# Splitting the first channel-mix weight's later parts into halves without TensorE, in a new order of work

## The chip, the cores and the metric

The kernel runs on one core of a Trainium2 chip. Its time is device time in microseconds (us) of one execution. Five engines work side by side, each through its own queue, in the order in which the program was built: PE (TensorE, matmul), DVE (VectorE), ACT (ScalarE), POOL (GpSimd) and SP, which here issues the transfers. PEld is the weight load of a matmul, which overlaps the matmul before it.

## The reference, cut to what matters

```python
# 1. linear attention with a decaying state, heads of 48, 768 steps, 4 batches
y[t] = r[t] @ (state + outer(u * k[t], v[t]));  state = w[t] * state + outer(k[t], v[t])
# 2. four experts of causal attention on x [4, 768, 384], the best two mixed by a gate
out += gate_e * softmax(mask((x@wq[e]) @ (x@wk[e]).T / 8)) @ (x@wv[e]) @ wo[e]
# 3. channel mix, what the change is about: w_ch1 is [384, 1536], w_ch2 is [1536, 384]
xn = (x - mean) / sqrt(var + 1e-6) * g_ln
return x + maximum(xn @ w_ch1, 0) @ w_ch2
```

## The kernel before, in words

Every large product is made of three float16 products: a float32 operand is scaled by a power of two and split into a high half (`hi`, the value rounded to float16) and a low half (`lo`, the rest), and hi x hi, hi x lo and lo x hi are summed. So the two channel-mix weights, w1 (w_ch1) and w2 (w_ch2), have to be split once, before the first block of rows can be multiplied by them.

Rows are worked in chunks of 128 (6 in each of 4 batches). A chunk passes the linear attention (`rwkv_chunk`), the projections of its batch (`project`, L1124, and L1145, which takes the high half off again in PSUM), the scores (L1303, their exponentials split by L1361 on ACT and L1365 on DVE), the sum over values (L1388), the output projection (L1440, copied out by L1453) and then, in blocks of two chunks, the norm (`norm`: L1494 makes the high half on ACT, L1498 the low one on DVE, L1505 transposes both by DMA into a tile called xnT) and the channel mix (`mlp`: L1533 multiplies by w1 into a tile called pm, L1544 and L1548 split the result, L1566 multiplies by w2 into pz, L1573 adds it to the rows). Block (0,0) is the first of twelve. In the names, numbers behind a tile are batch, chunk or buffer.

The weights arrive as 64-bit words. `big_weights` takes w1 in four groups of three parts and w2 in six groups of two; a part is 128x384. A group is loaded (L553) into a ring that later carries rows: w1 into the three slots of the ring of x1, the rows themselves (its tile is printed as x or x1_69), so that a group fills the ring, and w2 into the two slots of xnT. Three integer operations on DVE turn its words into float32 (`unpack`, L505 to L507). ACT then squares it for the largest value (`top`, L576). The scales of all weights come from the first groups alone, in one chain of small steps (`was`; their tile is s_all_False, and for w1 gsFalse).

From there a part can go two ways. By **TensorE**, for all of w1 and for w2's first group: PE multiplies the float32 part by a diagonal matrix of scales (`times`, L656, which goes over the data in two passes), ACT copies the product out as the high half (`hi`, L660), PE takes that off in PSUM (`less`, L664), ACT copies out the low half (`lo`, L668). The ring slot is free after `top`. Or **direct**, for the other five groups of w2: the decoded float32 words stay in the ring slot, ACT makes the high half from them (L633), and one DVE operation with two inputs from SBUF makes the low half (L637). Here the slot is free only after that `lo`.

The order of the work isn't that of the text: every step is recorded with its engine, an assumed duration, what it comes after and which ring slot it takes and frees, and a planner (`Plan.order`) lays the steps out. Of the steps that could start within `LOOK` it takes the one with the lowest `due`, plus `LATE` times the delay; `due` is a sum of numbers from the table `PLACE`, by step and by group. While PE would stand idle early on, the planner puts in dummy matmuls (`spin`, L745), ruled by `UNTIL`, `SPAN`, `LEAST` and `GAP`. What the planner lays out is then fixed in each engine's queue. A second copy of the steps behind it serves inputs that the fast one can't hold; it isn't run here.

```python
direct = which in PRM["DIRECT"] and k > 0 and not safe
```

is the line that chooses the way of group k.

## Time and profile before

| | |
|---|---|
| three runs | 624.44, 626.21, 627.24 us (median 626.21) |
| profiled execution | 624.58 us, of which span 622.9 us |
| PE busy | 591.2 us (95%) |
| DVE busy | 431.1 us (69%) |
| ACT busy | 386.8 us (62%) |
| POOL busy | 153.9 us (25%) |
| mean granted clock of PE | 0.997 |

The span is the time from the first to the last recorded instruction; 1.7 us of the execution lie outside it. A busy share is a mean over stages: here the first fifth of the span, in which the weights are split and the first chunks go through all stages, looks different from the rest, so the stretches have to be read apart.

### The profile page before, as it was taken

To read this page: it belongs to the slowest core of one execution; us is meant where nothing else is said; L and a number is where in the kernel's file an instruction comes from. 1 tells how busy PE (TensorE), PEld (TensorE's weight loads), DVE (VectorE), ACT (ScalarE), POOL (GpSimd) and SP (SyncE) were. 2 spreads that over 40 slices of the span, in tenths; PEclk is the share of its full clock that TensorE was granted. 3 is DMA by queue.
4 is the path that set the end of the run, shared out by engine and by line. 5 is a ranking of instruction groups with operands and counts; after the bars stand their busy time and mean duration, and the time that the engine had idled before them with its cause. 6 is when DMAs were issued, how large, how long until landed. Compare 5 with 4: busy or idle time off the path is not lost.

```text
span 622.9 us, 16217 instructions
## 1 busy us (share of the span) xinstructions
PE 591.2 (95%) x6560; PEld 438.1 (70%) x6560; DVE 431.1 (69%) x817; ACT 386.8 (62%) x1059; POOL 153.9 (25%) x179
## 2 busy tenths in 40 slices
PE   6689888799999999999999999999999999999996
PEld 3566655577688867767777776777876768687783
DVE  6979898879898679689973689765564645442230
ACT  6298879966775686777646778655484745543120
POOL 5525233425453125055530045100000000000000
PEclk9999999999999999999999999999999999999999
DMA  8744674695986476699764579646238354532000
GB/s 279 266 145 162 196 183 138 132 246 114 181 229 141 94 143 175 125 214 243 146 124 97 96 196 180 102 73 124 48 43 178 69 114 75 98 65 59 14 15 29
DMA packets 151138, 83.32 MB, mean 134 GB/s; under 512 B 123664, under 2 KB 136720, under 8 KB 151056
## 3 DMA queue, kind: packets, MB, share of 16 engines
q1 hardware_dynamic: 151056, 82.21, 57.2%
q8 instruction: 53, 0.87, 0.6%
q14 instruction: 29, 0.24, 0.1%
HBM read 42.34 MB, written 4.72 MB: 76 GB/s over the span
## 4 chain that ended last, share of the span: by engine, by line
PE 72%; DVE 11%; ACT 9%; DMA 4%; issue 2%; SPq 1%; POOL 0%; ACTq 0%; DVEq 0%
PE pz L1566 21%; PE pm L1533 21%; PE pq L1124 6%; PE ps L1303 5%; PE po L1388 4%; PE pa L919 3%; PE px L1440 3%; PE py L969 2%; PE pv L1189 2%; DMA xnT<-in_w_dram 2%; PE py L955 2%; ACT ps L1345 2%; DMA seq<-in_seq_dram 1%; DVE hl L1365 1%; PE pd L984 1%
## 5 line engine op out<-in xcount | busy, mean ns | idle before, releaser
L1566 PE MATMUL pz<-w_w,hid 128*128 128x384 f16 x864 | 151.8, 326 | 0.0
L1533 PE MATMUL pm<-xnT,w_w 128*128 128x256 f16 x1296 | 150.9, 274 | 0.5 <-DVE hid L1548 0.5
L1533 PEld LDWEIGHTS <-w_w 128*128 128x128 f16 x1296 | 124.8, 98 | 19.7 <-issue 3.7
L1566 PEld LDWEIGHTS <-hid 128*128 128x128 f16 x864 | 81.5, 98 | 50.7 <-issue 2.0
L1544 ACT ACTIVATE hid<-pm 128x512 f16<-128x512 f32 x72 | 42.6, 593 | 62.3 <-PE pm L1533 62.3
L1365 DVE SCALAR_TENSOR_TENSOR hl<-ps,hl 128x512 f16<-128x512 f32 (+2 forms) x68 | 54.6, 811 | 35.1 <-ACT hl L1361 34.5
L1548 DVE SCALAR_TENSOR_TENSOR hid<-pm,hid 128x512 f16<-128x512 f32 x72 | 49.2, 685 | 37.0 <-ACT hid L1544 36.6
L1482 POOL TENSOR_TENSOR rs_y<-rs_v,half 128x2 f32<-128x2 f32 x12 | 8.4, 700 | 218.5 <-ACT rs_v L1478 218.5
L892 POOL TENSOR_SCALAR_AFFINE_SELECT am<-cb 128x512 f32<-128x512 f32 x48 | 44.7, 954 | 60.8 <-DVE cb L878 37.7
L1124 PE MATMUL pq<-xT,w_qk 128*128 128x256 f16 x432 | 50.8, 273 | 0.0
L1361 ACT ACTIVATE hl<-ps 128x512 f16<-128x512 f32 (+2 forms) x68 | 46.6, 694 | 1.3 <-DMA pt<-hl 0.4
L1124 PEld LDWEIGHTS <-w_qk 128*128 128x128 f16 x432 | 41.4, 98 | 7.7 <-issue 2.0
L1345 ACT ACTIVATE ps<-ps,bias 128x640 f32<-128x640 f32 (+1 forms) x32 | 26.2, 819 | 29.5 <-DVE ps L1316 27.9
L863 POOL TENSOR_TENSOR tok<-tok 128x384 f32<-128x384 f32 x19 | 22.5, 1182 | 84.9 <-DMA tok<-in_tok_dram 84.9
L1388 PEld LDWEIGHTS <-pt 128*128 128x128 f16 x1008 | 37.1, 98 | 5.2 <-issue 0.8
L834 POOL TENSOR_TENSOR rp<-seq,fw 128x512 f32<-128x512 f32 x24 | 31.5, 1313 | 36.1 <-DVE fw L817 34.1
L1388 PE MATMUL po<-vt,pt 128*128 128x64 f16 x1008 | 39.6, 193 | 0.2 <-DMA pt<-hl 0.2
L1345 ACT ACTIVATE ps<-ps,bias,scales 128x128 f32<-128x128 f32 (+3 forms) x64 | 37.7, 589 | 1.8
L1316 DVE TENSOR_SCALAR_CACHE_REDUCE ps<-ps,scales 128x640 f32<-128x640 f32 (+1 forms) x32 | 30.4, 951 | 11.7 <-PE ps L1306 11.4
L1573 DVE SCALAR_TENSOR_TENSOR x<-pz,ioutFalse,x 128x384 f32<-128x384 f32 x24 | 14.7, 613 | 31.9 <-PE pz L1566 31.8
L802 DVE TENSOR_TENSOR_SCAN bw<-seq,starts 128x516 f32<-128x516 f32 x24 | 35.4, 1476 | 0.8 <-DMA seq<-in_seq_dram 0.6
L926 DVE COPY_PREDICATED am<-above,pa 128x512 f32<-128x512 int8 x48 | 33.1, 719 | 0.3
(225 smaller groups left out, 1062.1 us busy)
## 6 DMA issues: line engine op xcount, KB each, us to landing
seq<-in_seq_dram SPq DMA_DIRECT2D x48, 256.0 KB, 4.6
tok<-in_tok_dram SPq DMA_DIRECT2D x19, 384.0 KB, 3.9
seq<-in_seq_dram SPq DMA_DIRECT2D x24, 258.5 KB, 3.3
seq<-in_seq_dram SPq DMA_DIRECT2D x24, 192.0 KB, 4.9
xnT<-in_w_dram SPq DMA_DIRECT2D x6, 768.0 KB, 4.9
x<-in_w_dram SPq DMA_DIRECT2D x4, 1152.0 KB, 7.2
out_dram<-x SPq DMA_DIRECT2D x24, 192.0 KB, 2.4
xk<-kd SPq DMA_DIRECT2D x16, 192.0 KB, 3.3
```

The costliest lines, as they stand in the source:

```text
L802: V.tensor_tensor_scan(t["bw"][:, NP * CW : 0 : -1], t["wT"][:, NP * CW : 0 : -1], starts[:, NP * CW : 0 : -1], 0.0, op0=OP.mult, op1=OP.max)
L892: G.affine_select(out=t["am"][:, j], in_=t["cb"].rearrange("p (h j) -> p h j", j=2)[:, :, j, None].to_broadcast([P, NP, P]), compare_op=OP ...
L926: V.copy_predicated(t["am"][:, j], above[:, None, :].to_broadcast([P, NP, P]), t["pa"][j].rearrange("p (h t) -> p h t", t=P))
L1124: T.matmul(h["pq"][:, :n].rearrange("p (c t) -> p c t", t=P), wt["qk"][:, lw, kk, mt * P : (mt + 1) * P], t["xT", c0 // 2][:, :, lx * KK + ...
L1345: A.activation(ps, ps, AF.Exp, bias=h["bias"][:, e : e + 1], scale=-1.0 if alone else t["x"]["esc"], accum_out=r["sums"][:, e : e + 1])
L1361: A.activation(part(u, heads, 0, W), view(heads, h, W, spot), AF.Copy, scale=2.0 ** 14)
L1365: V.scalar_tensor_tensor(out=part(u, heads, half_at, W), in0=view(heads, h, W, spot), scalar=2.0 ** 14, in1=part(u, heads, 0, W), op0=OP.m ...
L1388: T.matmul(r["po"][:, e * HD : (e + 1) * HD], u["pt"][:, (lp * len(heads) + k) * (i + 1) + kb, :], t["vt"][:, kb, lv, e * HD : (e + 1) * H ...
L1533: T.matmul(h["pm"][:, j * 256 : (j + 1) * 256].rearrange("p (c t) -> p c t", t=P), wt["w1"][:, KK * (f // 3) + kk, lw, f % 3 * P : (f % 3 ...
L1544: A.activation(hid[fp][:, 0], h["pm"], AF.Relu)
L1548: V.scalar_tensor_tensor(out=hid[fp][:, 1], in0=h["pm"], scalar=0.0, in1=hid[fp][:, 0], op0=OP.max, op1=OP.subtract)
L1566: T.matmul(h["po"][:, :DM], hid[fp][:, lh, c0 : c0 + P], wt["w2"][:, 2 * fp + j, lw, :], start=(fp + j + i == 0), stop=(fp == NF // 2 - 1 ...
```

## The change

One entry of the parameters, `DIRECT`, now names w1 as well as w2. So w1's groups 1 to 3, nine parts, go the direct way: nine L656 pairs and nine L664 on PE and nine L660 and nine L668 on ACT are gone, nine L633 on ACT and nine L637 on DVE are new. Group 0 of w1 and of w2 stay with TensorE. The three slots of x1 are now held until the low halves of a group are made, where `top` freed them before. All other parameters of the planner and every number of `PLACE` are different too, so that each engine's queue has a new order. Line numbers behind the table are one lower in the changed kernel (L637 is L636 there).

```diff
-PRM = dict(LOOK=0.0326, LATE=14146.9836, UNTIL=35.809, SPAN=5.4007, LEAST=0.144, GAP=2.97, LAND=2.3828, NPA=6, NQ=1, NCB=5, DIRECT=('w2',), NST=5)
+PRM = dict(LOOK=0.0, LATE=1150.6432, UNTIL=44.1537, SPAN=2.789, LEAST=0.6368, GAP=2.61, LAND=2.2113, NPA=6, NQ=1, NCB=5, DIRECT=('w1','w2'), NST=5)
 PLACE = {
-    ('av', 0, 0): -158057.83, ('av', 0, 1): -232158.2, ('av', 0, 2): -102859.22, ('av', 0, 3): -263757.53,
...
```

Counted over the program's main part, PE has 18 dummy matmuls (L745) where it had 10; apart from the steps named so far every engine has the same instructions as before.

The first place is ACT's queue around the first copy of finished rows into x1 (L1453 before, L1452 after; px is the output projection). Before, part 2, 3 and 9 of w1 are on their way through PSUM there (w1_ps is the PSUM tile of `times`):

```order
L660 ACTIVATE w_w1_132<-w1_ps2_False_1234 128x384
L1453 ACTIVATE x1_69,mv_0_0_1287<-px_0_0_1264,scales_0_351 128x384
L660 ACTIVATE w_w1_132<-w1_ps3_False_1256 128x384
L1457 ACTIVATE mv_0_0_1287<-mv_0_0_1287 128x1
L1461 ACTIVATE spare_128,mv_0_0_1287<-x1_69,mv_0_0_1287 128x384
L812 ACTIVATE decay_120<-bw_1_0_1289 128x4
L668 ACTIVATE w_w1_132<-w1_ps2_False_1234 128x384
L1330 ACTIVATE bias_0_2_0_1330<-top_0_2_0_1306,scales_0_351 128x2
L668 ACTIVATE w_w1_132<-w1_ps3_False_1256 128x384
L1345 ACTIVATE ps_0_2_0_1278,sums_0_2_1335<-ps_0_2_0_1278,bias_0_2_0_1330,scales_0_351 128x384 x2
L660 ACTIVATE w_w1_132<-w1_ps9_False_1333 128x384
```

and now the queue has group 3's square (`top`) and its three high halves ahead of that copy, and nothing from PSUM of w1:

```order
L575 ACTIVATE w_w1_132,w1_maxFalse_136<-x1_69 128x1152
L1195 ACTIVATE vt_0_780<-pv_0_4_1234 128x256
L632 ACTIVATE w_w1_132<-x1_69,gsFalse_424 128x384
L1199 ACTIVATE lg_0_138<-pv_0_4_1234,scales_0_362 128x4
L822 ACTIVATE seq_0_5_910,sums_117<-seq_0_5_910,shift_118 128x4x128
L632 ACTIVATE w_w1_132<-x1_69,gsFalse_424 128x384 x2
L1329 ACTIVATE bias_0_2_0_1285<-top_0_2_0_1274,scales_0_362 128x2
L1344 ACTIVATE ps_0_2_0_1251,sums_0_2_1287<-ps_0_2_0_1251,bias_0_2_0_1285,scales_0_362 128x384 x2
L1360 ACTIVATE hl_0_2_0_1305<-ps_0_2_0_1251 128x768
L1452 ACTIVATE x1_69,mv_0_0_1307<-px_0_0_1264,scales_0_362 128x384
```

What moved: the PSUM copies of w1 that stood before, between and behind the copies into x1 are gone, and the three high halves stand ahead of the first copy, since x1's slots hold the group until its low halves are made.

The second place is DVE's queue at the same point. Before, DVE is done with w1 after its last decode (L507 into w_w1) and goes on to a group of w2 (L505 to L507 from xnT):

```order
L507 SCALAR_TENSOR_TENSOR w_w1_132<-x1_69,w_w1_132 128x1152
L1365 SCALAR_TENSOR_TENSOR hl_0_1_2_1107<-ps_0_1_2_1042,hl_0_1_2_1107 128x512
L505 TENSOR_SCALAR w_w2_133<-xnT_70 128x768
L1076 SCALAR_TENSOR_TENSOR xT_0_2_1116<-py_0_4_1003,scales_0_351,xT_0_2_1116 128x384
L1406 RECIPROCAL den_0_1_1114<-den_0_1_1114 128x4
L1407 TENSOR_TENSOR den_0_1_1114<-den_0_1_1114,gw_0_855 128x4
L808 RECIPROCAL begin_100<-bw_0_5_1092 128x4
L506 SCALAR_TENSOR_TENSOR w_w2_133<-xnT_70,w_w2_133 128x768
L507 SCALAR_TENSOR_TENSOR xnT_70<-xnT_70,w_w2_133 128x768
```

and now the three low halves of group 3 stand in one row ahead of the split of chunk 2's exponentials (hl_0_2_0):

```order
L1320 TENSOR_REDUCE top_0_2_0_1274<-ps_0_2_0_1251 128x2
L678 TENSOR_REDUCE sane_134<-w1_maxFalse_136 128x1
L680 TENSOR_SCALAR sane_134<-sane_134,g_peakFalse_135 128x1
L681 TENSOR_SCALAR sane_134<-sane_134,s_all_False_415 128x1
L682 TENSOR_SCALAR sane_134<-sane_134 128x1
L636 SCALAR_TENSOR_TENSOR w_w1_132<-x1_69,gsFalse_424,w_w1_132 128x384 x3
L801 SCALAR_TENSOR_TENSOR bw_1_0_1303<-seq_1_0_1199,starts_71 128x516
L1364 SCALAR_TENSOR_TENSOR hl_0_2_0_1305<-ps_0_2_0_1251,hl_0_2_0_1305 128x768
```

What moved: sixteen low halves (seven of w2 and nine of w1) now stand ahead of the low half of block (0,0)'s norm (L1498, L1497 after) where nine of w2 stood, and one group of w2 fewer is decoded ahead of it: nine groups instead of ten.

The third place is SP's queue. Before, the last group of w2 is loaded (L553, from in_w2) ahead of the transposes of chunk 2 and of block (0,0)'s rows (L1505):

```order
L553 DMA xnT_70<-in_w2_dram 128x768
L1429 DMA_TRANSPOSE oT_0_1_1291<-o16_0_1_1273 128x4x128
L773 DMA seq_1_1_1366<-in_seq_dram 128x517
L797 DMA tok_1_1_1379<-in_tok_dram 128x768
L781 DMA seq_1_1_1366<-in_seq_dram 128x512
L785 DMA seq_1_1_1366<-in_seq_dram 128x512
L1374 DMA_TRANSPOSE pt_0_2_0_1402<-hl_0_2_0_1361 128x12x128
L789 DMA seq_1_1_1366<-in_seq_dram 128x384
L1374 DMA_TRANSPOSE pt_0_2_2_1475<-hl_0_2_2_1453 128x12x128
L1505 DMA_TRANSPOSE xnT_70<-x16_0_0_1501 128x12x128
```

and now that load stands behind them, among the transposes of chunks 3 and 4, and waits for PE, since block (0,0)'s xnT has to be read out of the slots first:

```order
L784 DMA seq_1_3_1869<-in_seq_dram 128x512
L788 DMA seq_1_3_1869<-in_seq_dram 128x384
L1373 DMA_TRANSPOSE pt_0_4_0_1987<-hl_0_4_0_1946 128x10x128
L1428 DMA_TRANSPOSE oT_0_3_2015<-o16_0_3_1993 128x4x128
L552 DMA xnT_70<-in_w2_dram 128x768
L1373 DMA_TRANSPOSE pt_0_4_1_2100<-hl_0_4_1_2047 128x10x128
```

What moved: the last group of w2 is loaded, decoded and split after the last L1533 of block (0,0) instead of ahead of its first.

## Rows read from the trace of the kernel before

**Rows 1.** The page: busy time, share and instructions of each engine.

```profile
PE 591.2 (95%) x6560; PEld 438.1 (70%) x6560; DVE 431.1 (69%) x817; ACT 386.8 (62%) x1059; POOL 153.9 (25%) x179
```

**Rows 2.** Busy time by stretch (start:end length, PE, PEld, DVE, ACT, POOL, clock, DMA).

```profile
0.00:122.64 122.64, 98.71 (x996) 67.72 (x997) 105.94 (x214) 93.93 (x293) 50.67 (x61) 1.00 0.62 188
122.64:617.98 495.34, 492.48 (x5564) 370.35 (x5563) 325.11 (x603) 292.86 (x767) 103.28 (x118) 1.00 0.57 121
...
67.46:115.03 47.57, 39.78 (x461) 25.61 (x461) 43.20 (x84) 41.83 (x122) 17.99 (x19) 1.00 0.59 160
115.03:157.00 41.97, 39.61 (x515) 29.64 (x513) 34.87 (x62) 29.06 (x79) 14.38 (x15) 0.96 0.77 173
124.00:128.00 4.00, 4.00 (x41) 1.98 (x43) 3.47 (x7) 0.95 (x3) 0.00 (x0) 0.60 0.92 206
```

**Rows 3.** What PE waited for behind the first L1533: total, times, longest.

```profile
PE ps L1303 <- DVE hl L1365: 0.9, 3, 0.4
```

**Rows 4.** Timeline of block (0,0)'s way to PE, and the last L1573.

```profile
115.03 0.96 DVE L1498 TENSOR_TENSOR x<-xn,x 128x768 f16<-128x768 f32 x1 [0.17 <-ACT x L1494]
...
122.64 0.27 PE L1145 MATMUL pq<-kd,minus 128*128 128x256 f16 x1 [2.01 <-ACT kd L1138]
...
122.75 1.57 PE L1533 MATMUL pm<-xnT,w_w 128*128 128x256 f16 x11
...
617.36 0.62 DVE L1573 SCALAR_TENSOR_TENSOR x<-pz,ioutFalse,x 128x384 f32<-128x384 f32 x1 [5.23 <-PE pz L1566]
```

**Rows 5.** Groups by line and form: busy us, mean ns, idle before.

```profile
L656 PE MATMUL w_ps_False<-w_w,diag_w_False 128*128 128x384 f32 x24 | 9.8, 505 | 0.3 <-ACT w_w L668 0.3
...
L664 PE MATMUL w_ps_False<-w_w,minus 128*128 128x384 f16 x14 | 4.3, 327 | 1.2 <-ACT w_w L660 1.0
...
L633 ACT ACTIVATE w_w<-xnT,s_all_False 128x384 f16<-128x384 f32 x10 | 6.4, 654 | 0.0
...
L660 ACT ACTIVATE w_w<-w_ps_False 128x384 f16<-128x384 f32 x14 | 7.1, 518 | 0.5 <-PE w_ps_False L656 0.5
...
L637 DVE SCALAR_TENSOR_TENSOR w_w<-xnT,s_all_False,w_w 128x384 f16<-128x384 f32 x10 | 5.8, 609 | 1.4 <-ACT w_w L633 1.4
...
L505 DVE TENSOR_SCALAR w_w<-xnT 128x768 int32<-128x768 int32 x6 | 4.3, 712 | 5.8 <-DMA xnT<-in_w_dram 5.8
...
L506 DVE SCALAR_TENSOR_TENSOR w_w<-xnT,w_w 128x768 int32<-128x768 int32 x6 | 6.0, 1000 | 0.1
...
L507 DVE SCALAR_TENSOR_TENSOR xnT<-xnT,w_w 128x768 int32<-128x768 int32 x5 | 5.5, 1110 | 0.1
...
L802 DVE TENSOR_TENSOR_SCAN bw<-seq,starts 128x516 f32<-128x516 f32 x24 | 35.4, 1476 | 0.8 <-DMA seq<-in_seq_dram 0.6
```

**Rows 6.** Timeline of two PE pieces of the split.

```profile
84.45 1.46 PE L656 MATMUL w_ps_False<-w_w,diag_w_False 128*128 128x384 f32 x4
...
90.67 0.33 PE L664 MATMUL w_ps_False<-w_w,minus 128*128 128x384 f16 x1
```

**Rows 7.** What DVE waited for up to 115 us: total, times, longest.

```profile
DVE w_w L505 <- DMA xnT<-in_w_dram: 5.8, 2, 3.4
DVE w_w L637 <- ACT w_w L633: 1.4, 1, 1.4
```

**Rows 8.** The page, issues: KB each, us to landing.

```profile
xnT<-in_w_dram SPq DMA_DIRECT2D x6, 768.0 KB, 4.9
```

**Rows 9.** Timeline: two DVE operations with and without POOL beside them.

```profile
30.31 0.96 DVE L507 SCALAR_TENSOR_TENSOR xnT<-xnT,w_w 128x768 int32<-128x768 int32 x1
...
76.99 0.61 DVE L637 SCALAR_TENSOR_TENSOR w_w<-xnT,s_all_False,w_w 128x384 f16<-128x384 f32 x1
...
77.36 1.09 POOL L873 TENSOR_TENSOR tok<-tok,u_sb 128x384 f32<-128x384 f32 x1 [0.37 <-DMA u_sb<-in_ub_dram]
...
89.00 1.00 POOL L863 TENSOR_TENSOR tok<-tok 128x384 f32<-128x384 f32 x1 [3.98 <-DMA tok<-in_tok_dram]
...
89.10 1.72 DVE L507 SCALAR_TENSOR_TENSOR xnT<-xnT,w_w 128x768 int32<-128x768 int32 x1
```

51 lines of the change are left out of this document (25 added, 26 removed), and 79 rows, old and new, of the table PLACE.

## The prediction, made before the changed kernel had run

> **What bounds the kernel now.** I read the page's busy line first: PE 591.2 us of 622.9, DVE 431.1, ACT 386.8 [rows 1]. That mean hides two stages, so I cut the span where TensorE starts its first L1533, at 122.64 us, and where the last result is added, at 617.98 (a start of 617.36 and 0.62 of length) [rows 4]. Behind the cut PE is busy 492.48 us of 495.34; ahead of it only 98.71 of 122.64 [rows 2]. The list of PE's waits says the same of the later stage: the largest is 0.9 us in all, on DVE's L1365 [rows 3]. So from 122.64 us on the time is PE's work, and the change has nine parts less of that only if they stand there. Ahead of it PE has 24 us of holes, and the question is what lets the first L1533 start.
>
> That is the way of block (0,0): DVE's low half L1498 at 115.03, the transposes, then L1533 at 122.75, right behind an L1145 for which PE had idled 2.01 us [rows 4]. On the way to L1498 I compare DVE and ACT: from 67.46 us (the first low half of the exponentials) to 115.03 DVE is busy 43.20 of 47.57 us, ACT 41.83 and PE 39.78 [rows 2]. DVE is the fullest there, with 4.4 us idle, and ACT follows close behind. So a step taken from PE or ACT helps as far as DVE waited for it, and a step given to DVE costs its whole length.
>
> **Removed, PE.** Two parts by L656 took 1.46 us, with a tail of pipeline in it [rows 6]; by the means, a pass starts while the last one drains, and I count 0.65 us a part, 0.16 for L664 (half of the 0.33 that one takes alone with its tail [rows 6]): 9 x 0.81 = 7.3 us. All nine stand ahead of the first L1533 in the old order, and all five that are left do in the new one. Summed over the rows of PE's queue ahead of the first L1533, work falls by 5.0 us, with the eight new dummy matmuls counted in (these cost nothing as long as PE has holes; that cover is 24 us). Behind it the sum falls by only 0.5 us. **So the removal itself is worth 0.5 us**, and the rest has to come from an earlier first L1533.
>
> **Removed and added, ACT.** Nine L660 at 0.518 [rows 5] and nine L668, about as long, go: 9.3 us. Nine L633 at 0.654 come: 5.9 us. ACT is 3.4 us lighter, all of it ahead of block (0,0).
>
> **Added, DVE.** Nine L637 at 0.609 [rows 5]: 5.5 us on the fullest engine. This is the part that speaks against the change. But the new order also moves work. Ahead of L1498 there are now 16 L637 instead of 9: +4.3 us. One group of w2 is decoded behind it, not ahead: 0.71 + 1.00 + 1.11 = 2.8 us less [rows 5]. Some sixteen other lines change by a step or more, most by under 0.5 us; the largest is one scan L802 less, 1.5 us [rows 5]; together they take off 2.6 us. **DVE's work ahead of L1498 so changes by +4.3 - 2.8 - 2.6 = -1.1 us.**
>
> **The start of the full stretch.** If DVE idles there as long as before, L1498 comes 1.1 us earlier. If lighter ACT and PE close all the holes of the last stretch, it gains 4.4 us more: 5.5. Between these ends I take the middle, since half of the neighbours' relief is in PE, for which DVE seldom waits: **-3.3 us**. From L1498 to L1533 nothing on the way changes, so I keep its 7.7 us.
>
> **The last group of w2.** Its load now stands behind block (0,0)'s last L1533, for its slots hold that block's xnT. By the old rows' durations along PE's new queue, that comes 23.3 us of PE work behind the first L1533, and the first matmul that needs this group comes at 37.0. In between lie the load, 4.9 us [rows 8], the decode of 2.8, two L633 and the last L637 (1.3 + 0.6): 9.6 us against 13.7. The transfer fits. DVE's queue is tighter: in the 41.97 us behind L1498 DVE is busy 34.87 [rows 2], so in 44.6 us (7.6 to the first L1533 and 37.0 behind) some 37.1; with 2.8 of decode and two L637 of 1.2 that is 41.1. If DVE idles as much as before there (7.5 us), PE waits 4.0 us; if the new work fills the holes, nothing. I take **+1.5**, nearer to the filled case, because DVE there mostly waits for PE's results, with work in hand for the group in those holes.
>
> **The sum.** -3.3 - 0.5 + 1.5 = -2.3 us. The profiled execution took 624.58, so it would read 622.3; it is 1.6 below the median of the runs, 626.21, which becomes **623.9 us**. With the ends, -5.5 - 0.5 + 0 = -6.0 and -1.1 - 0.5 + 4.0 = +2.4: 620.2 to 628.6.
>
> **Rival: the whole gain comes through.** The holes close, L1498 comes 5.5 us earlier and the last group of w2 is hidden: 620.2. One thing could add to it: behind the 2.01 us in which PE idled, the granted clock over the next four microseconds was 0.60 [rows 2, 4], between the two levels of 1.2 and 2.4 GHz, which costs 0.4 x 4.0 = 1.6 us. If the new order leaves no hole there, 1.6 to 3.6 us more: 616.6. For it: ACT loses 3.4 us of work and PE the longest dependent chain of the early stage (product, copy, product, copy). Against it: DVE has no less of its own work than 1.1 us under the old.
>
> **Rival, slower: low halves that wait for their high halves.** Each L637 needs the L633 just made by ACT, and DVE's queue stands still until it is there; behind the three of group 3 stand a scan and chunk 2's exponentials hl_0_2_0, for which PE's L1388 waits, and the ring of x1, so the first L1453. One of the ten old pairs did wait, 1.4 us [rows 7]. Nine new pairs are made while ACT is 88% busy (41.83 of 47.57 [rows 2]). With n of nine waiting 1.4 us, the start moves by 1.4 n: from n = 4 on the sum of -2.3 is past +3.1 (that is 0.5% of the time, about what a measurement of this kernel can tell from no change); at n = 5 it is +4.7, **630.9 us**. Against it: nine of ten old pairs had no wait, and the high halves stand early in ACT's queue.
>
> **Rival: new DVE operations stretched by POOL.** An L507 took 0.96 us alone and 1.72 where POOL worked on L863 at the same time; but an L637 kept its 0.61 though POOL's L873 began within it [rows 9]. If the seven more that stand ahead of L1498 stretch like that L507, by 0.79 of 0.61, that is 0.48 each: 3.4 us if all meet POOL, 1.3 at POOL's share of 17.99 in 47.57 [rows 2]. The time is then 625.2 to 627.3, no change. The Trainium skill (SBUF — State Buffer, section "SBUF: two separate sides") states such a rule: a VectorE operation with two SBUF inputs and a GpSimd one share a pair of ports as an exclusive lock, and the loser waits for the whole instruction. By that rule, which the stretched L507 bears out and the one L637 does only in so far as it had begun first, the way through PSUM that is given up was the one with no claim on the ports.
>
> **How the numbers follow.** Forecast 0.48, of which 0.15 lies beyond 3.1 us faster and 0.33 within 0.5%. The whole gain 0.23, all faster. Low halves that wait 0.18: 0.17 slower, 0.01 within. Stretched by POOL 0.11: 0.08 within and 0.03 slower. So faster 0.38, same 0.42, slower 0.20. The range has to take in the forecast's ends and most of the two outer rivals: 617.5 to 630.5, with about 0.1 left out on each side.
>
> **What would show it.** In the new trace: L1497 (the old L1498) at 109.5 to 114 and the first L1532 some 7.7 us behind it; PE's work behind that unchanged, so that the end moves with it; the waits of PE behind the first L1532, with L1565 waiting for DVE's L636 by 0 to 4 us; DVE's waits for L632 ahead of L1497, below 3 us if I am right and 5 or more for the slower rival; the length of the L636 beside POOL. I am wrong if the first L1532 isn't earlier than 121.5, if PE loses over 4 us behind it, or if PE's later work changes by more than the 0.5 us, for instance by a clock that falls again.

## The result, and the profile after

The changed kernel took 633.37 us in the median of four runs (630.99 to 635.59), the one before 626.15 beside it. The ratio is 1.0115, with a 95% interval of 1.0094 to 1.0136: **slower by 7.2 us**, where 623.9 was forecast, and beyond the range's 630.5. The profiled execution is the longest of the four, 635.59 us, 11.0 more than that of before, so its pieces below add up to more than the median does.

The page of the changed kernel, its busy line and the granted clock in 40 slices:

```profile
PE 593.2 (94%) x6541; PEld 436.3 (69%) x6541; DVE 440.3 (69%) x826; ACT 385.6 (61%) x1050; POOL 147.6 (23%) x179
...
PEclk9578887989999999999999999999999999999999
```

Against [rows 1] ACT is 1.2 us lighter and DVE 9.2 us heavier, and PE, with 19 instructions fewer, is busy 2.0 us longer. The second line points to why: in the first fifth the granted clock is below full in most slices. By stretch, changed kernel (columns as in [rows 2]: length, PE, PEld, DVE, ACT, POOL, clock, DMA share, GB/s):

```profile
0.00:131.30 131.30, 102.04 (x995) 68.01 (x996) 110.82 (x216) 92.41 (x277) 46.89 (x60) 0.82 0.57 170
131.30:627.67 496.37, 491.17 (x5549) 368.26 (x5546) 329.44 (x610) 293.21 (x775) 100.67 (x119) 1.00 0.57 122
44.00:52.00 8.00, 7.23 (x50) 4.95 (x50) 6.48 (x10) 4.85 (x13) 1.50 (x2) 0.57 0.32 103
76.00:80.00 4.00, 3.84 (x13) 1.72 (x12) 3.83 (x10) 3.19 (x11) 1.93 (x3) 0.50 0.89 214
104.00:112.00 8.00, 5.45 (x50) 2.87 (x51) 7.80 (x13) 6.59 (x22) 3.23 (x3) 0.50 0.26 50
128.00:132.00 4.00, 4.00 (x51) 2.98 (x49) 2.46 (x7) 1.89 (x7) 0.00 (x0) 0.73 0.69 148
```

The cut at the first L1532 (L1533 before) shows where most of the loss is. Behind it the stretch is 496.37 us long where it was 495.34: +1.0, the size that was forecast (-0.5 + 1.5). (That cut takes 122.64 us from the forecast; by [rows 4] it is the start of the L1145 ahead, and the first L1533 starts at 122.75.) Ahead of it are 131.30 us where there were 122.64. The remaining 1.1 us come after the last addition, in the write to memory: the span ends 6.0 us behind the end of that addition, where it was 4.9; the profiles below have 4.9 to 6.4 there, in either order. So between these two profiles nearly the whole surprise lies ahead of the first L1532. The way of block (0,0) there, timeline of DVE and POOL around the norm's low half L1497, and the starts of L1532 and of the last L1572:

```profile
119.11 1.00 POOL L862 TENSOR_TENSOR tok<-tok 128x384 f32<-128x384 f32 x1 [5.68 <-DMA tok<-in_tok_dram]
119.44 1.49 DVE L1497 TENSOR_TENSOR x<-xn,x 128x768 f16<-128x768 f32 x1
120.19 1.59 POOL L872 TENSOR_TENSOR tok<-tok,u_sb 128x384 f32<-128x384 f32 x1
120.85 1.34 DVE L636 SCALAR_TENSOR_TENSOR w_w<-xnT,s_all_False,w_w 128x384 f16<-128x384 f32 x1
...
131.30 0.38 PE L1532 MATMUL pm<-xnT,w_w 128*128 128x256 f16 x2
...
627.05 0.62 DVE L1572 SCALAR_TENSOR_TENSOR x<-pz,ioutFalse,x 128x384 f32<-128x384 f32 x1 [5.23 <-PE pz L1565]
```

L1497 comes at 119.44, 4.4 us later than in [rows 4] and not 3.3 earlier, and the first L1532 is 11.9 us behind it, not 7.7.

The transposes of block (0,0)'s rows aren't what the first L1533 waited for, in either kernel. Before, they were issued at 116.58 us and had landed 4.0 us later, 2.2 us ahead of it:

```profile
116.58 1.42 SPq L1505 DMA_TRANSPOSE xnT<-x  x1
...
DMA to landing us min/median/max: 4.0/4.0/4.0
```

In the changed kernel they were issued at 120.95 and landed after 3.7, 6.7 us ahead of the first L1532. The chain that the profile follows back from it runs another way, from DVE's maximum of the scores (L1321) through ACT's exponentials to its copy kd (L1138) and PE's L1145. Before:

```profile
118.33 1.24 DVE top L1321
...
119.92 0.88 ACT ps L1345 x2
...
122.21 0.39 ACT kd L1138
...
122.64 0.27 PE pq L1145
122.91 2.90 PE pm L1533 x18
```

and in the changed kernel, where that step is L1144 and other work (projections, L1123, and linear attention, L936 to L970) stands in PE's queue between it and the first L1532:

```profile
122.53 1.14 DVE top L1320
...
126.65 0.28 ACT kd L1137
...
126.97 0.37 PE pq L1144
127.34 1.98 PE pq L1123 x9
129.32 1.22 PE py L968 x24
130.55 0.22 PE py L970 x8
130.76 0.59 PE pk L936 x4
131.35 0.11 PE pq L1144
131.46 0.98 PE pm L1532 x9
```

So of the 8.5 us by which the first L1532 is late, 4.3 lie up to that L1144 (126.97 against 122.64) and 4.2 in PE's queue behind it (4.33 us against 0.11). L1498 counts in the old order because DVE reaches L1321 through the same queue, 3.3 us behind it.

DVE's busy time up to L1497 tells more than either number:

```profile
0.00:119.44 119.44, 94.48 (x909) 62.48 (x910) 100.55 (x195) 86.21 (x258) 41.98 (x56) 0.81 0.57 176
```

For the kernel before, the same view up to its L1498:

```profile
0.00:115.03 115.03, 93.45 (x936) 63.61 (x937) 99.25 (x200) 86.88 (x272) 48.26 (x58) 1.00 0.62 192
```

DVE's work grew by 1.3 us, its idle time by 3.1 (15.78 to 18.89). The forecast had 1.1 less work and no more idle time. (In e6_after_fill below, where DVE's queue is the same, the work is 99.30 and the idle time 17.45: profiles of one queue differ by over 1 us.) Part of the idle time is in the list of what DVE waited for (20 to 126 us, changed kernel; total, times, longest):

```profile
DVE w_w L636 <- ACT w_w L632: 5.2, 5, 2.1
```

And PE waited, before its lower stretches, for 1.8 to 2.4 us at a time (timeline of the changed kernel; the wait is the bracket at the row's end):

```profile
42.80 0.66 PE L936 MATMUL pk<-ident,k 128*128 128x128 f32 x4 [1.82 <-DVE k L828]
...
76.16 0.83 PE L1302 MATMUL ps<-kd,qs 64*128 64x256 f16 x6 [1.76 <-DVE hl L1364]
...
102.74 0.49 PE L918 MATMUL pa<-rp,k 48*128 48x128 f32 x2 [2.39 <-POOL rp L833]
...
126.11 0.27 PE L1144 MATMUL pq<-qs,minus 128*128 128x256 f16 x1 [1.76 <-ACT qs L1137]
```

Behind each of these four the granted clock reads lower: 0.57 of full over 44 to 52 us, 0.50 over 76 to 80, 0.50 over 104 to 112, 0.73 over 128 to 132. A reading of 0.50 is the lower of the two levels, 1.2 of 2.4 GHz. That it is no fault of the reading shows in the matmuls themselves, one line's over 44 to 52 us (ns, least, median and most; first and last start). Changed kernel:

```profile
L954 PE MATMUL py<-rp,dec x24: 420/421/423, 49.6 to 50.7; 128*32 128x128 f32 x24
```

and the same line in the kernel before:

```profile
L955 PE MATMUL py<-rp,dec x24: 272/273/297, 47.0 to 47.6; 128*32 128x128 f32 x24
```

So three suspects stand side by side: the halves themselves (work on ACT and DVE, with waits between them), the clock (PE no longer fills its pauses), and the new order. The experiments had to part them.

### The profile page after: what moved, and what is told of

Read it like the earlier page. It is cut to its first block, busy times and chain, and to the rows that moved or that the text cites. A ratio compares the mean times of both kernels' runs of the same rounds, so it can differ in the third digit from the quotient of the medians.

```text
span 633.7 us, 16168 instructions
## 1 busy us (share of the span) xinstructions
PE 593.2 (94%) x6541; PEld 436.3 (69%) x6541; DVE 440.3 (69%) x826; ACT 385.6 (61%) x1050; POOL 147.6 (23%) x179
## 4 chain that ended last, share of the span: by engine, by line
PE 69%; DVE 12%; ACT 9%; DMA 4%; issue 4%; POOL 1%; SPq 0%; ACTq 0%; DVEq 0%; POOLq 0%
PE pz L1565 19%; PE pm L1532 17%; PE pq L1123 6%; PE ps L1302 4%; PE po L1387 4%; PE pa L918 3%; PE pv L1188 3%; PE px L1439 3%; PE py L968 2%; DMA pt<-hl 2%; PE py L954 2%; ACT ps L1344 2%; DVE bw L801 1%; DVE hl L1364 1%; DVE w_w L636 1%
## 5 line engine op out<-in xcount | busy, mean ns | idle before, releaser
L1565 PE MATMUL pz<-w_w,hid 128*128 128x384 f16 x864 | 151.0, 326 | 0.3 <-DVE w_w L636 0.3
L1532 PE MATMUL pm<-xnT,w_w 128*128 128x256 f16 x1296 | 150.8, 273 | 0.0
L1532 PEld LDWEIGHTS <-w_w 128*128 128x128 f16 x1296 | 124.5, 98 | 16.2 <-issue 0.6
L1565 PEld LDWEIGHTS <-hid 128*128 128x128 f16 x864 | 81.8, 98 | 51.9 <-issue 2.1
L1123 PE MATMUL pq<-xT,w_qk 128*128 128x256 f16 x432 | 52.3, 277 | 2.2 <-DVE vt L1203 1.8
L891 POOL TENSOR_SCALAR_AFFINE_SELECT am<-cb 128x512 f32<-128x512 f32 x48 | 39.2, 839 | 58.0 <-DVE cb L877 33.7
L862 POOL TENSOR_TENSOR tok<-tok 128x384 f32<-128x384 f32 x19 | 22.1, 1163 | 122.7 <-DMA tok<-in_tok_dram 122.7
L1123 PEld LDWEIGHTS <-w_qk 128*128 128x128 f16 x432 | 42.0, 99 | 9.6 <-issue 3.7
L1572 DVE SCALAR_TENSOR_TENSOR x<-pz,ioutFalse,x 128x384 f32<-128x384 f32 x24 | 14.7, 612 | 31.1 <-PE pz L1565 30.9
L801 DVE TENSOR_TENSOR_SCAN bw<-seq,starts 128x516 f32<-128x516 f32 x24 | 33.5, 1394 | 1.6 <-DMA seq<-in_seq_dram 1.6
```

The lines of the kernel that those rows point to most:

```text
L801: V.tensor_tensor_scan(t["bw"][:, NP * CW : 0 : -1], t["wT"][:, NP * CW : 0 : -1], starts[:, NP * CW : 0 : -1], 0.0, op0=OP.mult, op1=OP.max)
L891: G.affine_select(out=t["am"][:, j], in_=t["cb"].rearrange("p (h j) -> p h j", j=2)[:, :, j, None].to_broadcast([P, NP, P]), compare_op=OP ...
L1123: T.matmul(h["pq"][:, :n].rearrange("p (c t) -> p c t", t=P), wt["qk"][:, lw, kk, mt * P : (mt + 1) * P], t["xT", c0 // 2][:, :, lx * KK + ...
L1532: T.matmul(h["pm"][:, j * 256 : (j + 1) * 256].rearrange("p (c t) -> p c t", t=P), wt["w1"][:, KK * (f // 3) + kk, lw, f % 3 * P : (f % 3 ...
L1565: T.matmul(h["po"][:, :DM], hid[fp][:, lh, c0 : c0 + P], wt["w2"][:, 2 * fp + j, lw, :], start=(fp + j + i == 0), stop=(fp == NF // 2 - 1 ...
```

## The experiments

### First group: one setting back at a time

Four kernels undo one of the change's parts and let the planner lay the order out again: the way of w1 in the new order and in the old one, and two settings of the dummies.

e1_neworder_olddirect, the new table with the old way of w1:

```diff
-DIRECT=('w1','w2')
+DIRECT=('w2',)
```

> The changed kernel with one word taken back: w1 goes through TensorE again, the new tables and planner settings stay. Three theories. (D) The direct way of w1 costs the time, through DVE's nine low halves and x1's slots that are held longer: then this comes back to 625 to 628 us. (O) The new order costs it, since it puts the split of the q and k weights and the first projections later (first L1123 at 52.3 us, 40.2 before): then 631 us or more, for those stand in the same order here. (K) TensorE's clock costs it, which was at half in 44 to 51, 74 to 82 and 103 to 113 us of the changed kernel: then nine pieces more on TensorE keep it busier, a mean clock above 0.98 and 626 to 629 us.

Measured: 645.97 us, ratio 1.031 (1.0268 to 1.0352).

e2_oldorder_newdirect, the old table with the new way:

```diff
-DIRECT=('w2',)
+DIRECT=('w1','w2')
```

> The kernel before with one word added: w1's groups 1 to 3 go direct, all its old tables and planner settings stay, so that nearly all other work keeps its order. (D) expects 631 to 634 us. (O) expects 624 to 627 us, by my prediction's own terms: 0.5 us less TensorE work and 1.5 to 4 us more DVE work ahead of block (0,0). (K) expects TensorE to lose nine pieces and the mean clock to fall below 0.985, with 628 to 632 us.

Measured: 663.47 us, ratio 1.0594 (1.0554 to 1.0634).

e3_after_oldspin, the changed kernel with the old settings of the dummies:

```diff
-UNTIL=44.1537, SPAN=2.789, LEAST=0.6368, GAP=2.61
+UNTIL=35.809, SPAN=5.4007, LEAST=0.144, GAP=2.97
```

> The changed kernel with the old rules for the dummy matmuls alone (10 instead of 18, as in the kernel before). If the new placing of the dummies is what loses the clock, this is 626 to 629 us with a clock above 0.98. (O) and (D) expect no change, 631 to 635 us. If the eight more dummies did help, it is slower than the changed kernel by 0.5 to 2 us.

Measured: 647.29 us, ratio 1.0344 (1.0299 to 1.0388).

e5_after_spinall, the changed kernel with dummies in every pause up to 125 us:

```diff
-UNTIL=44.1537, LEAST=0.6368, GAP=2.61
+UNTIL=125, LEAST=0, GAP=0.25
```

> The changed kernel with some eighty dummy matmuls in TensorE's planned waits up to 125 us, 0.22 us each, so that TensorE has no long pause and its clock should stay at the upper level. (K) expects most of the 7.2 us back: 624 to 628 us, first L1532 before 124 us. (O) and (D) expect the late steps to be late all the same: 630 to 636 us though the clock is above 0.985.

Measured: 652.42 us, ratio 1.0418 (1.037 to 1.0466).

All four missed: they take 13 to 37 us more than the kernel whose table they keep. One setting changes the start of some steps, and the planner then lays out everything behind them anew with a table that fits other starts. They isolate nothing, and none is used below. From here on the laid-out order of one of the two kernels is kept, and single steps are put into it, moved or taken out.

### Second group: pauses of PE filled with dummies

e6_after_fill keeps the order of the changed kernel and puts 52 dummy matmuls into eight of its pauses, those above among them (a name, its group, its how-manieth step, and how many dummies ahead of it):

```diff
+    ('mm_k', ('rw', 2), 1): 6,
+    ('mm_s', ('s', 0, 1), 2): 6,
+    ('mm_v', ('vals', 0, 2), 1): 6,
+    ('mm_a', ('rw', 5), 1): 8,
+    ('mm_o', ('o', 0, 1), 1): 10,
+    ('mm_v', ('vals', 0, 2), 2): 4,
+    ('mm_q', ('proj', 0, 2), 7): 6,
+    ('q_less', ('proj', 0, 2), 2): 6,
```

> The changed kernel in its own order, with 52 dummy matmuls put into eight of TensorE's measured pauses between 41 and 127 us (6 ahead of the third L936, 6 ahead of L1302 at 76.2, 6, 8, 10, 4, 6 and 6 ahead of L1188, L918, L1439, L1188, L1123 and L1144 at 97.1, 102.7, 107.3, 116.4, 122.6 and 126.1); nothing else moves. Behind five of these pauses the clock fell to its lower level. (K) If the clock costs the time, it stays at the upper level here behind 45 us, the first L1532 comes 4 to 8 us earlier and the time is 626 to 629 us. (O) If the order costs it by its waits alone, the clock is up and the time is 632 to 635 us, the dummies lying in waits or adding to them.

Measured: 630.82 us in the median beside 625.71 of before; ratio 1.0121 (1.0087 to 1.0155). Two of its six runs are at 635.2 and 635.6, four at 629.4 to 631.3; the ratio counts them all. In its profile the clock is at full level in the middle of the front (windows of e6_after_fill):

```profile
40.00:52.00 12.00, 10.86 (x121) 7.51 (x119) 10.17 (x16) 10.10 (x30) 3.29 (x3) 1.00 0.55 166
68.00:76.00 8.00, 4.84 (x58) 2.99 (x58) 6.51 (x17) 6.87 (x25) 2.40 (x3) 1.00 0.93 270
104.00:112.00 8.00, 6.78 (x109) 4.20 (x107) 7.69 (x13) 6.35 (x22) 4.64 (x5) 1.00 0.47 111
```

and the first L1532 starts at 125.98 where it was 131.30, the last L1572 at 622.03 where it was 627.05. So the fall of the clock can be cured, with 5.3 us between these two profiled executions at the first L1532. Not all of that is the clock's: ahead of the first added dummy, at 39.4 us, e6's profile already is 1.4 us the earlier one (the first L1075 stands at 28.39 against 29.81), and it is the fastest of its six runs (629.42) where the changed kernel's is the slowest of four. In the time it is less certain: 2.1 us by the medians (each against its own runs of before: 7.2 and 5.1 above them), nothing by the ratios.

e7_before_fill puts eight dummies into the 2.01 us ahead of L1145 in the kernel before [rows 4]:

```diff
+    ('q_less', ('proj', 0, 2), 4): 8,
```

> The kernel before with eight dummy matmuls ahead of the one L1145 for which TensorE paused 2.01 us at 120.6, behind which the clock read 0.60. (K) expects no fall there and 1 to 1.6 us less: 624.6 to 625.2 us. If such a fall is hidden, nothing changes: 626 us. If the dummies get in the way, 0.5 to 1 us more.

Measured: 625.39 us, ratio 0.9993 (0.9975 to 1.0011). In the time that stretch at 0.60 was worth nothing that can be measured. The profile says more. The clock is at full level behind the first L1533, and the stretch from there to the last addition takes 493.52 us where it took 495.23 (from 122.75 us on):

```profile
124.88:618.40 493.52, 490.76 (x5564) 369.86 (x5562) 325.24 (x603) 293.23 (x767) 101.72 (x118) 1.00 0.58 121
```

But L1498 stands at 117.16 in it, 2.1 us later than in the kernel before, though nothing was edited ahead of it. So profiles of one and the same queue can lie 2 us apart, and differences of that size in the table below aren't sure.

f1_after_fill_early adds 30 dummies in the first 36 us to e6, f2_before_fill_early 32 to the kernel before, e7's eight among them:

```diff
+    ('mm_intra', ('rw', 0), 1): 16,
+    ('o2', ('small',), 1): 8,
+    ('mm_k', ('rw', 1), 1): 6,
```

> The changed kernel with the 52 dummies in its later pauses and 30 more in the three early ones (16 ahead of the first L968 at 17.5 us, 8 ahead of the second L434, 6 ahead of the second L936), so that TensorE has the upper clock from 10 us on. If the early half-rate stretch (16 to 39 us) is what is left of the 7 us, 626 to 628 us and the second L1075 at 41 to 42 us instead of 43.4. If the order itself is, 629 to 631 us.

Measured: 643.03 us, ratio 1.0269 (1.0244 to 1.0294).

```diff
+    ('mm_k', ('rw', 0), 1): 3,
+    ('mm_intra', ('rw', 0), 1): 16,
+    ('o2', ('small',), 1): 5,
```

> The kernel before with 32 dummies in its pauses (3 ahead of the first L937, 16 ahead of the first L969, 5 ahead of the second L435, 8 ahead of the L1145 at 122.6). If TensorE's half rate up to 33 us delays its front too, the L969 there take 0.28 us instead of 0.42 and the time is 623 to 625 us, faster than both kernels; if DVE sets the front alone, 625 to 626.5 us.

Measured: 630.44 us, ratio 1.0066 (1.0041 to 1.0091). In both the dummies stood in the way: at the lower level the sixteen of f2 took 10.23 us, the first chunk behind them came 4.9 us later, and the time is 4.8 us longer. So what PE does at the lower level in the first 36 us was not tested; f2 shows only that a delay that early comes through to the end at about its full length.

### Third group: the change in the old order

e8_before_direct keeps the order of the kernel before and takes nine parts of w1 off TensorE. Their high and low halves stand right behind their group's square, the load of the next group behind them:

```diff
+    times.gone = less.gone = True
...
+            o.start = tops[k].end + 0.65 * (j + (what == "lo")) + (0.1 if what == "lo" else 0.0)
...
+            o.start = tops[o.set[1] - 1].end + 0.65 * 3 + 0.2
```

> The order of the kernel before, kept step by step, with w1's groups 1 to 3 direct: their nine L656, L664, L660 and L668 are gone, each group's three L633 and three L637 stand right behind its square, and the loads of groups 2 and 3 behind those. So this is the change without the new order. (D) If the direct way costs the time, 631 to 636 us. (O, K) If it is the order and the clock falls that it brings, this is 623 to 628 us: TensorE has 7.3 us less in a stage where it idles anyway and DVE 5.5 us more, so I expect 626 to 628 and the first L1533 between 122 and 126 us.

Measured: 635.44 us, ratio 1.0152 (1.0122 to 1.0182). Its windows:

```profile
40.00:52.00 12.00, 9.46 (x67) 6.61 (x65) 8.78 (x11) 8.12 (x23) 3.51 (x3) 0.78 0.64 207
68.00:76.00 8.00, 5.97 (x54) 4.80 (x52) 6.90 (x20) 6.46 (x24) 2.66 (x4) 0.74 0.37 112
...
116.00:124.00 8.00, 4.64 (x38) 2.88 (x38) 7.42 (x13) 6.75 (x20) 3.75 (x4) 0.72 0.76 193
```

With the old order kept, the clock falls as in the changed kernel. So it isn't the new order alone that opens the pauses.

e9_before_direct_dummies is e8 with three dummies where each L656 pair stood and one for each L664:

```diff
-    times.gone = less.gone = True
+    times.dummy, less.dummy = 3, 1
```

> The old order with w1's groups 1 to 3 direct, as in the run before it in this document (635.4 us), but TensorE keeps its load: where a removed L656 pair stood there are three dummy matmuls (0.65 us) and for a removed L664 one. So only ACT's and DVE's part of the change is left, and the rings. If TensorE's clock (K) is the cause, because the nine removed pieces had filled its pauses, the time comes back to 626 to 629 us and no long stretch reads 0.5. If DVE's added work and the later loads are the cause (D), it stays at 633 to 636 us.

Measured: 631.61 us, ratio 1.011 (1.007 to 1.015). The same windows of e9:

```profile
40.00:52.00 12.00, 9.52 (x111) 6.39 (x113) 9.92 (x13) 9.66 (x26) 3.82 (x3) 1.00 0.73 247
68.00:76.00 8.00, 7.65 (x102) 4.50 (x99) 6.32 (x20) 4.96 (x21) 1.22 (x2) 1.00 0.81 195
...
116.00:124.00 8.00, 6.46 (x84) 4.84 (x85) 7.21 (x20) 7.81 (x24) 4.34 (x5) 1.00 0.53 114
```

The clock is back, and the first L1533 moves from 134.11 to 128.43 us (0.8 of it already ahead of the first added dummy, at 42.3 us). In the time e9 stands 0.4% below e8, with intervals that overlap. So here too the clock's share in the time, some 2.6 us by the ratios, isn't settled; what is settled is that 1.1% remain where the profile shows no dip of the clock from 40 us on.

### Fourth group: the halves left out

These kernels leave out one or both halves of the nine parts; the matmuls are the same in number and shape. The square of each group writes its result where a half is missing, so that other, finite numbers stand there; in g1 and g2 the high half's place is read for both halves.

e10_e9_no_low and e13_e9_no_high are e9 without its nine low or its nine high halves:

```diff
-    for x in sorted(new, key=lambda x: x.start):
+    for x in sorted((x for x in new if getattr(x, 'moved', 'l')[0] != 'lo'), key=lambda x: x.start):
```

> The same, without the nine new L637 on DVE: the low halves of those nine parts are left out (they hold other, finite numbers), and x1's slots are free after the high halves. Against the kernel with them this prices DVE's 5.5 us and the waits for the high halves. (D) expects 5 to 9 us less than that kernel. If DVE isn't what holds the early stage, 0 to 2 us less.

Measured: 632.53 us, ratio 1.0103 (1.0074 to 1.0133).

```diff
-    for x in sorted(new, key=lambda x: x.start):
+    for x in sorted((x for x in new if getattr(x, 'moved', 'l')[0] != 'hi'), key=lambda x: x.start):
```

> The old order, w1's groups 1 to 3 direct, dummies for TensorE's removed pieces (631.6 us), without the nine high halves on ACT. If ACT's three 0.65-us pieces right behind each square hold up what ACT has next (the splits of the q, k and value weights), the time comes back to 626 to 627.5 us. If it is something else (DVE's low halves, the late loads), 630 to 632 us.

Measured: 630.21 us, ratio 1.0064 (1.0035 to 1.0094).

e11_fill_no_low and e12_fill_no_high are the same for e6:

```diff
-                    done[part] = lo
+                    done[part] = lo; lo.skip = which == "w1"
```

> The changed kernel with its pauses filled by dummies (630.8 us), without its nine L636 of w1: these low halves are left out. What is left is the new order with less work on DVE, ACT and TensorE than the kernel before. If the remaining 5 us are DVE's low halves, this is 624 to 627 us. If they are the order's, 629 to 631 us.

Measured: 631.73 us, ratio 1.0097 (1.0061 to 1.0132).

```diff
+                    hi.skip = which == "w1"
```

> The changed kernel with its pauses filled by dummies (630.8 us), without its nine L632 of w1 on ACT: these high halves are left out (they hold other, finite numbers), the nine L636 stay and no longer wait for them. If ACT's high halves, and DVE's waits for them, are what the new order pays for, 624 to 627 us. If not, 629 to 631 us, as leaving out the low halves brought nothing there.

Measured: 631.09 us, ratio 1.0087 (1.006 to 1.0114). None of the four differs surely from its parent. Had I stopped here, the halves would have seemed to cost nothing. g1_new_order_no_halves and g2_old_order_no_halves leave out both, in e6 and in e9:

```diff
+                    hi.skip = which == "w1"
-                    done[part] = lo
+                    done[part] = lo; lo.skip = which == "w1"
-                                     wt["w1"][:, KK * (f // 3) + kk, lw, f % 3 * P : (f % 3 + 1) * P], q["xnT"][:, :, lx * KK + kk, :],
+                                     wt["w1"][:, KK * (f // 3) + kk, 0, f % 3 * P : (f % 3 + 1) * P], q["xnT"][:, :, lx * KK + kk, :],
```

> The new order with its later pauses filled by dummies (630.8 us), without any splitting of w1's groups 1 to 3: both the nine L632 and the nine L636 are left out (the high half's place holds other, finite numbers and is read for both halves). TensorE, ACT and DVE then have less work ahead of block (0,0) than in the kernel before. If it is the new order as such that is slow, this stays at 629 to 632 us. If one of the two engines always stood in for the other when only one half was left out, it falls to 624 to 627 us.

Measured: 629.11 us, ratio 1.0044 (1.0029 to 1.0059).

```diff
-    for x in sorted(new, key=lambda x: x.start):
+    for x in sorted((x for x in new if not hasattr(x, 'moved')), key=lambda x: x.start):
```

> The same in the old order: w1's groups 1 to 3 neither through TensorE nor direct, dummies where TensorE's removed pieces stood, so only the decode and the squares are left of them. Against the old order with the direct way (631.6 us) this prices the two halves together. If they are all of its 6 us, 624 to 626 us, at or below the kernel before; if more than 628, the order with direct pieces taken out has another cost that I have not named.

Measured: 624.97 us beside 626.46, ratio 0.9979 (0.9964 to 0.9993). This is the row that matters most. The old order with neither the halves nor the nine parts' copies from PSUM on ACT, and dummies on PE in place of the pieces, is 0.2% faster than the kernel before: with the split of nine parts for nothing, **only some 1.3 us were to be had** there. In the profiles the first L1533 doesn't move at all (122.70 against 122.75); what g2 gains lies behind it, where its clock didn't fall (493.78 us, as e7). And with both halves put back (e9) it is 1.3% slower, with intervals far apart. So the halves together cost 1.3% there, 8.2 us, and at least 0.77% (4.8 us) by the intervals' ends.

That price takes in what the halves do to x1's slots. The load of w1's group 3 starts at 61.64 us in g2 and at 67.88 in e9, 66.58 in e13, 67.13 in e10 and 71.73 in e8, where the slots are held longer, and in these four DVE waits for it once, 0.6 to 2.3 us. In e9:

```profile
73.91 0.76 DVE L505 TENSOR_SCALAR w_w<-x 128x1152 int32<-128x1152 int32 x1 [1.01 <-DMA x<-in_w_dram]
```

No kernel of the old order has the halves without the late load, and none moves the load alone that far, so the two aren't parted; and each of e10 and e13 still has the late load.

What each kernel does to DVE up to L1498 (L1497 in the new order), from the windows of each trace, idle being the start less the busy time; the clock is the mean from 40 us to the first L1533 (why from 40 on is told at the end):

| kernel | order | halves of w1's nine parts | low half starts | DVE busy ahead | DVE idle ahead | first L1533 | clock |
|---|---|---|---|---|---|---|---|
| before | old | by TensorE | 115.03 | 99.25 | 15.8 | 122.75 | 1.00 |
| g2 | old | none | 114.97 | 100.04 | 14.9 | 122.70 | 1.00 |
| e13 | old | low only | 121.67 | 107.03 | 14.6 | 129.40 | 0.96 |
| e10 | old | high only | 122.97 | 100.62 | 22.4 | 130.69 | 0.94 |
| e9 | old | both | 120.71 | 106.64 | 14.1 | 128.43 | 1.00 |
| e8 | old | both, no dummies | 126.39 | 108.16 | 18.2 | 134.11 | 0.87 |
| g1 | new | none | 116.64 | 94.54 | 22.1 | 125.86 | 1.00 |
| e11 | new | high only | 116.72 | 93.91 | 22.8 | 125.94 | 1.00 |
| e12 | new | low only | 117.09 | 98.61 | 18.5 | 126.30 | 1.00 |
| e6 | new | both | 116.75 | 99.30 | 17.5 | 125.98 | 1.00 |
| after | new | both, dummies as planned | 119.44 | 100.55 | 18.9 | 131.30 | 0.85 |

Two readings follow. **In the old order** nine low halves put 6.6 us on DVE (g2 to e9), and L1498 moves by 5.7: there DVE has no room, as the forecast had read from [rows 2]. With high halves alone (e10) DVE has no more work but 7.5 us more idle time. So taking the low halves away gains nothing as long as the high ones stand there: the loss isn't additive. How much of e10's idle time is ACT's queue and how much the clock, 0.94 in its profile, isn't separated.

**In the new order** the clock is full in four of the five, and they agree to within half a microsecond: in these profiles the halves do nothing to the start. Taking both away (e6 to g1) frees DVE of 4.8 us, and all of it turns into idle time. There, DVE's work doesn't set L1497. The time of g1 is nevertheless below that of e6, by 2.5 us in the medians (2.7 and 5.1 above their own runs of before), by at least 0.28% (1.8 us) between the intervals' ends. The two profiles can't show that gain: e6's is its fastest run, 629.42, and g1's, 629.16, is near its median. Where it lies stays open.

The order alone can be read between g1 and g2, which ran on the same chip and have the same work but for dummies: 1.0044 against 0.9979, 4.1 us, at least 0.36% (2.3 us) by the intervals' ends. In the profiles the first L1533 lies 3.2 us later in g1, and the low half 1.7. The low half's 1.7 don't reach it: DVE's L1320 behind it starts at 118.45 us in g1 and L1321 at 118.28 in g2, PE's L1144 that waits for kd at 122.90 and L1145 at 122.59. So 0.3 us lie up to there, and 2.9 are the other work that stands behind that L1144 in PE's queue, as in the changed kernel above. Behind the first L1533 g1 loses 2.2 us more. The two stretches to the last addition, g2 and then g1 (columns as before: length, PE, ...):

```profile
122.70:616.48 493.78, 490.98 (x5564) 369.76 (x5562) 325.14 (x603) 293.21 (x767) 103.02 (x118) 1.00 0.57 121
125.86:621.85 495.99, 490.35 (x5549) 368.68 (x5546) 330.04 (x612) 293.10 (x775) 101.35 (x119) 1.00 0.57 123
```

PE is busy 0.6 us less there and idles for 5.64 us instead of 2.80. Among its waits in g1 are two that g2 doesn't have:

```profile
PE po L1387 <- DMA pt<-hl: 1.4, 2, 0.8
PE px L1439 <- DMA oT<-o: 1.2, 1, 1.2
```

So it is in every profile: in those of the new order (changed kernel, e6, e11, e12, f1, g1) PE idles 5.2 to 7.4 us behind the first L1532, in those of the old order (before, e7 to e10, e13 to e15, f2, g2) 2.6 to 3.3.

### Fifth group: ACT and the loads by themselves

e15_before_more_act leaves the kernel before as it is and adds nine copies of a 128x384 part on ACT, behind the squares where e8 has its high halves:

```diff
+    x.run = lambda: A.activation(spare, fulls[which][:, part], AF.Copy, saturate=False)
...
+        o.start = tops[o.moved[1]].end + 0.65 * o.moved[2]
```

> The kernel before as it is, through TensorE, with nine copies more on ACT, 128x384 each, three behind the square of each of w1's groups 1 to 3, whose results nobody reads. If ACT's queue at these three places is what costs the time, 629 to 632 us; if ACT's holes take them, 625 to 626.5 us.

Measured: 632.99 us, ratio 1.011 (1.0059 to 1.0162). The copies, by form in its trace:

```profile
L1769 ACT ACTIVATE spare<-w_w x9: 511/530/622, 43.0 to 99.6; 128x384 fp8e4<-128x384 f32 x9
```

Nine at 0.53 are 4.8 us of work, and the time rose by 6.9. Nobody waits for what they write. ACT, 62% busy on the page, has no room at these places of its queue. In this profile too the clock is below full (0.93 from 40 us to the first L1533), so part of the 6.9, at least the 2 us above the copies' own length, may be the clock's.

e14_before_late_loads moves only the loads of w1's groups 2 and 3 back to where e8 has them:

```diff
+            o.start = tops[o.set[1] - 1].end + 0.65 * 3 + 0.2
```

> The kernel before as it is, through TensorE, with one thing of the change: the loads of w1's groups 2 and 3 are issued some 2.2 us later, at the place that they have when x1's slots wait for the low halves (46 and 68 us instead of 42.6 and 61.1). If the late loads are the cost, 628 to 631 us; if DVE has other work meanwhile, 625 to 626.5 us.

Measured: 625.97 us, ratio 1.0013 (0.9993 to 1.0034). The loads started at 43.3 and 62.1 us, hardly later than in the kernel before (42.6 and 61.1), so it is a weak test: in e8 and e9 the second of these loads starts at 71.7 and 67.9 us, and the slots held that much longer are not shown to be harmless.

## Why the prediction was wrong, step by step

**What bounds the kernel now: right, as far as the later stretch goes.** That stretch is PE's, busy for 491.17 of its 496.37 us. In most kernels above the time follows the first L1533, not in all: in e7 it stands 2.1 us later than before and the last L1573 only 0.4, in g2 it doesn't move and the last L1573 comes 1.5 earlier.

**Removed, PE: the 0.5 us were small as said, but the cover was misjudged.** "These cost nothing as long as PE has holes" was told of the dummies; the other side is that the removed pieces had filled holes. Without them the clock falls, in the old order (e8) and in the new one. That the clock falling again would prove me wrong was written down, but as a last clause and without a price, while the rival for the faster side counted a gain from the clock. In the profiles it is 5.3 to 5.7 us at the first L1533, 0.8 to 1.4 of which stand ahead of any added dummy; in the time 2.1 to 2.6, with intervals that don't exclude nothing.

**Start of the full stretch: the term of -3.3 us is where the sum broke.** It measured +4.4 at L1497 and +8.5 at the first L1532. Three parts of it fell. DVE's work was to shrink by 1.1 us and grew by 1.3 (by 0.05 in e6). The lighter ACT was to close DVE's holes up to 4.4 us, and the holes grew by 3.1. And "nothing on the way changes" from L1498 to L1533: it became 11.9 us, 9.2 with the pauses filled. The way itself was misread: the transposes had landed 2.2 us before the first L1533 started, and what it waited for was the L1145 with its 2.01 us of idle time, that is ACT's kd L1138. In the new order other work stands between that step and the first L1532 in PE's queue, 4.2 us in the changed kernel and 2.9 in g1. The fault behind all of these is one: I added up work per engine where the chain goes from engine to engine, and credited ACT with a lighter load without asking at which places of its queue the new pieces stand and the old ones had stood. The removed copies from PSUM (L660, L668) cost next to nothing where they were: without those of the nine parts, and with no halves at all, g2 gains 0.2%. e15 shows 4.8 us of ACT's work at the places that e8 gives the high halves with a rise of 6.9.

**The ceiling was readable.** The forecast took up to 5.5 us for the start out of relief. g2 bounds that at 1.3 us in the old order. The profile before had said so in its way: DVE's waits ahead of L1498 [rows 7] name neither the pieces on PE nor their copies; in [rows 5] L664 waits for L660, 1.0 us in all, that is one piece of the split for another.

**The last group of w2: about right; the sum behind the first L1533 by luck.** L1565 waited once for the last low half (PE's waits from 115 us on, changed kernel):

```profile
PE pz L1565 <- DVE w_w L636: 0.3, 1, 0.3
```

0.3 us, at the low end of 0 to 4. The 0.5 us less of PE's work are borne out between g2 and g1 (0.6). That the later stretch grew by 1.0 = -0.5 + 1.5 is a coincidence of two things that the sum doesn't have: the kernel before took 1.3 to 1.7 us longer there in its profile, with the fall of the clock behind the first L1533, than its queue did in e7 and e14 (493.5 and 493.9 us, without the fall), and the new order idles PE there for 2.3 us more, for other steps than this one.

**Rival of low halves that wait: the sign came, but not from the new pairs.** DVE waited for L632 five times, 5.2 us in all, in the band named for that rival ("5 or more"). Four of the five, 4.8 us, are low halves of w2 (from xnT); of w1's nine one waited, 0.4 us. The longest of the four and that one:

```profile
60.41 0.62 DVE L636 SCALAR_TENSOR_TENSOR w_w<-xnT,s_all_False,w_w 128x384 f16<-128x384 f32 x1 [2.10 <-ACT w_w L632]
...
67.24 0.62 DVE L636 SCALAR_TENSOR_TENSOR w_w<-x,gsFalse,w_w 128x384 f16<-128x384 f32 x1 [0.39 <-ACT w_w L632]
```

g1, which has none of w1's halves, has the four waits of w2 all the same, 5.4 us in all. So the new order brings these waits (before there was one, of 1.4 us [rows 7]), not the nine pairs, and L1497 doesn't move when w1's are away. In the old order it is the other way round: the four waits of e9, 2.7 us, are all of w1's low halves.

**Rival of POOL: seen, and too small.** L1497 took 1.49 us beside POOL's L862 and L872 where it had taken 0.96 [rows 4], an L636 behind it 1.34 where its kind takes 0.61 [rows 5]: 1.3 us in all, both in the stretch ahead of the first L1532. In e6 the same L1497 took 0.95. The rule of the Trainium skill that the prediction cited (SBUF — State Buffer, section "SBUF: two separate sides") agrees with both rows in kind, not quite in size: L862 and L872 had 0.67 and 0.93 us left to run when L1497 and the L636 began, and these two took 0.53 and 0.73 longer.

**The order: not priced at all.** I read what moved by its sum and let the order itself count as neutral. It costs 4.1 us between g1 and g2, ahead of the first L1533 and behind it.

Together, by the medians of each kernel above its own runs of before: the order costs 2.7 us (g1), the halves in it 2.5 (e6 less g1), the clock 2.1 (the changed kernel less e6), 7.2 in all (they add up because each is the difference to the next; by the ratios they are 2.8, 4.8 and -0.4). The first has an interval of 1.8 to 3.7 us, the second is shown only to be over 1.8, the third not to be over nothing. What stays open is which steps of the new order make up its cost (the profiles show where it lies, no run moves a single step), what the halves cost without the late load of x1's slots, what the slow first 36 us are worth in either kernel, and the clock's exact share.

## What to carry to other kernels

Before crediting a removed operation, ask who waited for it: where no list of waits named it here, its removal gained next to nothing (nine parts' split: 1.3 us), and on PE it may have been what kept the clock up. Follow the chain back from the milestone before taking a distance on it as fixed: the 7.7 us from L1498 weren't the transposes'. Price an added operation by the place in its engine's in-order queue, not by the engine's busy share: 4.8 us on an engine that is 62% busy cost 6.9, the clock's part in it not parted. And leave out both of a pair in an experiment, not only one at a time: to leave out either half changed nothing for sure, to leave out both gave 1.3%, the earlier load among it.
